# First-layer tiles of one chunk, earlier weight loads, and attention steps held back in the first tile

## The chip, the cores and the metric

The kernel runs on one core of a Trainium2 chip. The metric is the device time of one execution in microseconds (us). In what follows PE is TensorE, DVE is VectorE, ACT is ScalarE, POOL is GpSimd, and SP is the engine that issues all DMA transfers in this kernel, one after the other.

## The reference

A decayed linear attention over chunks feeds two feed-forward layers. Cut to what matters:

```python
# x: (4 batches, 8 heads, 768 positions, 32), a: decay per position, B, C: state of 16
for each chunk of positions:
    M       = (C @ B.T) * exp(cum_i - cum_j) * causal
    y       = M @ x + (C @ state) * exp(cum)
    state   = exp(sum(log a)) * state + sum_j (B_j x_j) * decay_from_j
x = y as 3072 tokens x 256
h = max(x @ w1, x @ w2, x @ w3)          # 256 -> 768
x = h @ w_out                            # 768 -> 256
x = (sigmoid(x @ w_gate) * (x @ w_val)) @ w_out2     # 256 -> 1536 -> 256
```

The four first-layer matrices and the three second-layer matrices arrive as 8-byte floats, viewed as integers, and are decoded on the chip.

## The kernel before

**Attention.** The kernel takes chunks of 96 positions, 8 chunks in all; a chunk of all four batches is 384 tokens. One attention step treats four of the 32 (batch, head) pairs of a chunk, so a chunk has 8 steps and there are 64 steps in all. A step `k` is a product `s` on PE (line 280 for the first two chunks, line 283 later), a multiplication by the decays `mt` (DVE at line 295, or for every second step an ACT copy at 291 and POOL at 292), and a product `y` on PE (line 301). After four steps half a chunk is finished: ACT writes the high part `xt_hi` (line 310), DVE the remainder `xt_lo` (312) and four transposes that carry the state into the next chunk's `xs` (316). The decays of two steps come as one tile `dec`, which is broadcast by a DMA (line 213) into one of four buffers and turned into cumulative products by two scans on DVE (235). From the third chunk on, B and C are split into three bf16 parts (`split_bc`: ACT at 247, POOL at 256) and stored by 12 DMAs into `bi` and `cs` (252).

**First layer.** Tokens are cut into six tiles of 512 columns. A tile has six blocks `m`, and a block has three banks `u` (six matmuls each) and the down product of the block before, `o` (six matmuls). So a tile has 108 `u` and 36 `o` matmuls, each with its own weight load. A block is four slots: one per bank and one for the down product. At the end of every slot `slot_end()` starts attention steps towards a goal, so that the chunks of the next tile are ready in time, and lets waiting work take one stage (`tick`). Between PE's banks run the maxima (ACT 395, DVE 397 and 399), the high part `hi` (ACT 388) and the remainder `lo` (POOL 390).

**Weights.** Each block `m` has two pieces, `raw_a` m0 and m1, of two DMAs of 256 KB (line 127). A piece is decoded by three ACT instructions (141, 143, 144), two on DVE (`t_a` at 148, `r_a` at 150), a cast on ACT (155) and a subtraction on POOL (157). The first block of the first tile can't run before the first two pieces are decoded, and so on through the tile; later tiles find all 12 pieces in place. `BEHIND` says how many pieces are put on SP's queue behind which `dec`. By the page a `dec` is 388 KB, a chunk's `xs` 512, `bx` 256 and `bc` 448 KB, and the stores of a chunk's parts are six of 128 KB (`bi`) and six of 96 KB (`cs`).

**Order.** Every engine runs its instructions in the order that a scheduler gave them when the program was built. SP's queue is such an order too: a transfer that waits for a buffer to come free holds back all that stand behind it. `issue_after` tells the scheduler to place an instruction behind another one. The first 12 steps (`START`) run ahead of the first tile.

**Second layer.** Six tiles of 512, 12 blocks each, lines as in the first layer with `w_b`. It is the same in both kernels.

Of the kernel before, what the change touches and what calls it, by code (L numbers as in the profile page):

```python
# [7 lines left out]
F32 = mybir.dt.float32  # L8
F32R = mybir.dt.float32r
# [9 lines left out]
CH = 96  # L19
# [4 lines left out]
NT = NB * S  # L24
TT = 512
NTT = NT // TT
DM = NH * D
KD = DM // 128
FF1, FF2 = 768, 1536
# [8 lines left out]
TERMS = [(0, 0), (0, 1), (0, 2), (1, 0), (1, 1), (2, 0)]  # L38
KT = 16 * len(TERMS)
DEC = 512  # L40
START = 12
FIRST = 2 * NG
MASKED = 8
LEAD = 2
MTS = 5
DECS = 4

BEHIND = {4: 1, 5: 1, 6: 2, 7: 2, 8: 2, 9: 1, 10: 1, 11: 1, 12: 1}


class Pipe:
# [15 lines left out]
def scan_attention_then_ffn(ctx: ExitStack, tc: tile.TileContext, xh, ah, bch, pick, bn, w1, w2, w3,  # L67
# [170 lines left out]
    def split_bc(c):  # L238

        r = awk.tile([128, BW + 384], F32, tag="bc", bufs=1, name=f"bc{c}")  # L240
        sp.dma_start(out=r, in_=bch[:, c])
        parts = awk.tile([128, 3, BW + 384], BF16, tag="parts", bufs=1, name=f"parts{c}")
        cs[c] = awk.tile([KT, NU, CH], BF16, tag="cs", name=f"cs{c}")
        yield
        for p in range(3):
            with tc.issue_after(evict[0].ins) if c > 2 else ExitStack():
                act.copy(parts[:, p], r)
            for k, (dst, cols) in enumerate(((bi[c % 2], slice(0, BW)),
                                             (cs[c], slice(BW, BW + 384)))):
                for t, pr in enumerate(TERMS):  # L250
                    if pr[k] == p:
                        sp.dma_start(  # L252
                            out=dst[16 * t:16 * t + 16].rearrange("n (g q) i -> n g (q i)", q=4),
                            in_=parts[:, p, cols])
            if p < 2:
                pool.tensor_tensor(out=r, in0=r, in1=parts[:, p], op=ALU.subtract)
            yield splits if p == 2 else None
# [6 lines left out]

    def need(t):

        return 4 * -(-(t + 1) * TT // (2 * CH))

    def attention(k, ahead):

        c, g = steps[k]
        m = mt[k % MTS]
        if k < FIRST:
            ck = cm[:, k % MASKED]
            act.mul(ck.rearrange("p q i -> p (q i)"), bcf[c][:, BW:], pk[:, g:g + 1])
        ps = psu.tile([128, 4, 128], F32, tag="up", name=f"s{c}_{g}")
        for q in range(4):
            u = 4 * g + q
            if k < FIRST:
                pe.matmul(ps[:, q, 0:CH], bcf[c][:, 128 * q:128 * q + 128], ck[:, q],  # L280
                          start=True, stop=True)
            else:
                pe.matmul(ps[:, q, 0:CH], bi[c % 2][:, u, :], cs[c][:, u, :],  # L283
                          start=True, stop=True)
        for _ in range(ahead + 1):
            yield
        dc = dec[k // 2][:, 4 * (g % 2):4 * (g % 2) + 4]
        pool.tensor_tensor(out=m[:, :, CH:CH + N], in0=bx[c][:, 4 * g:4 * g + 4, :],
                           in1=dc[:, :, CH:LW].to_broadcast([128, 4, N]), op=ALU.mult)
        if k >= 4 and k % 2 == 0:  # L290
            act.copy(m[:, :, 0:CH], ps[:, :, 0:CH])
            pool.tensor_tensor(out=m[:, :, 0:CH], in0=m[:, :, 0:CH], in1=dc[:, :, 1:LW],
                               op=ALU.mult)
        else:
            last[0] = dve.tensor_tensor(out=m[:, :, 0:CH], in0=ps[:, :, 0:CH], in1=dc[:, :, 1:LW],
                                        op=ALU.mult)
        prepare(k)
        yield
        y = ys[g // 4]
        for q in range(4):  # L300
            pe.matmul(y[32 * q:32 * q + 32, g % 4, 0:CH + N], xs[c][:, 4 * g + q, :], m[:, q, :],  # L301
                      start=True, stop=True)
        if g % 4 == 3:
            yield
            h = g // 4
            o = (c * CP + 2 * CH * h) % RING
            src = y[:, :, 0:CH].rearrange("p (b k) i -> p b k i", k=KD)
            hi, lo = (v[:, :, o:o + 2 * CH].rearrange("p k (b i) -> p b k i", b=2)
                      for v in (xt_hi, xt_lo))
            act.copy(hi, src)  # L310
            yield
            dve.tensor_tensor(out=lo, in0=src, in1=hi.bitcast(F32), op=ALU.subtract)  # L312
            if c + 1 < NC:
                for q in range(4):
                    rows = slice(32 * q, 32 * q + 32)
                    dve.transpose(
                        out=xs[c + 1][rows, 16 * h:16 * h + 16, :].rearrange(
                            "p (g q) d -> p g q d", q=4)[:, :, q, :],
                        in_=y[rows, :, CH:128])

    def prepare(k):

        c, g = divmod(k, NG)
        if g == 0 and 0 < c < NC - 1:
            load_x(c + 1)
            splits.append(split_bc(c + 1))
        if splits and next(splits[0], None) is splits:
            splits.pop()
        n = k // 2
        if k % 2 == 0:  # L330
            if 5 <= n + 4 < NC * NP:
                load_decay(n + 4, ad)
        elif k < 9:
            decay(n + 1, n == 0)
        else:
            for i in ([n + 1] if k == 9 else []) + [n + 2]:
                if i < NC * NP:
                    with tc.issue_after(last[0].ins) if k > FIRST else ExitStack():
                        decay(i)

    def att_step(ahead=0):
# [12 lines left out]
    acc = {}  # L354

    def down(t, m, mn, w, hl, finish):
        if m == 0:
            acc[t] = [psos[t % len(psos)].tile([128, TT], F32, tag=f"o{d}", name=f"o{mn}_{t}_{d}")
                      for d in range(KD)]
        first = len(w) - KD  # L360
        for d in range(KD):
            three(acc[t][d], [m], mn, w, lambda k: first + d, lambda k: hl[0], lambda k: hl[1])
        if m == mn - 1:
            pipe.add(finish(t, acc[t]))

    def finish1(t, ps):
        yield
        for d in range(KD):
            act.copy(y1[:, d, t * TT:(t + 1) * TT], ps[d])

    def finish2(t, ps):
        yield
# [39 lines left out]
        chain.tick()  # L412
        pipe.tick()

    def layer(t, m, w, n, stages):

        o = (t * TT) % RING
        s = tmpp.tile([128, TT], F32, tag="s", bufs=3, name=f"s{n}_{t}_{m}")
        hl = [tmpp.tile([128, TT], F32R, tag=h, name=f"{h}{n}_{t}_{m}") for h in ("hi", "lo")]
        banks = []  # L420
        for j in range(n):
            ps = psu.tile([128, TT], F32, tag="up", name=f"u{n}_{t}_{m}_{j}")
            three(ps, range(KD), KD, w, lambda k: KD * j + k,
                  lambda k: xt_hi[:, k, o:o + TT], lambda k: xt_lo[:, k, o:o + TT])
            banks.append(ps)
            if j == 0:
                chain.add(stages(s, banks, hl))
            yield hl
# [9 lines left out]
    next(store_all, None)  # L438
    load_x(0, slice(0, 16))
    load_decay(1, ah)  # L440
    load_decay(2, ad)
    load_x(0, slice(16, 32))
    sp.dma_start(out=bcf[1], in_=bch[:, 1])
    load_decay(3, ad)
    load_x(1, slice(0, 16))
    load_decay(4, ad)
    decay(0, clip=True)
# [15 lines left out]

    def slot_end():
        t, s = divmod(slot, slots)
        if t + 1 < NTT:
            goal = need(t) + (need(t + 1) - need(t)) * (s + 1) / (slots - 5)
            while done[0] < min(goal, need(t + 1)):
                for _ in range(2 if t > 1 else 1):
                    att_step(1 if t > 1 else 0)  # L470
        tick()
        weights_tick(t < NTT - 1 or s % 3 == 2)

    for t in range(NTT):
        for m in range(M1):
            for hl in layer(t, m, wt1[m], 3, most):
                slot_end()
                slot += 1
            if pend is not None:
                down(*pend)  # L480
            slot_end()
            slot += 1
            pend = (t, m, M1, wt1[m], hl, finish1)
            if t == NTT - 1 and m == 0:
                actx.close()
                wp2.append(ctx.enter_context(tc.tile_pool(name="wp2", bufs=1)))
                psos.append(ctx.enter_context(tc.tile_pool(name="pso2", bufs=1, space=PSUM)))
                todo += [(piece2, m, part) for m in range(M2) for part in range(2)]
                while todo:
                    load_weights()  # L490
            if t == NTT - 1 and m in (2, 4):
                pipe.add(split_y(m // 2 - 1))


# [1 line left out]
    order += [(t, m) for t in range(2, NTT) for m in range(M2)]  # L496
    for t, m in order:
        eng = pool if t < 2 else dve
        for hl in layer(t, m, wt2[m], 2, lambda s, b, h: gated(s, b, h, eng)):
            tick()  # L500
            slot += 1
            weights_tick(slot % 3 == 2)
# [77 lines left out]
```

## Time and profile before

| | |
|---|---|
| median of three runs | 581.92 us (579.84 to 582.04) |
| the profiled execution's own time | 582.93 us |
| its span, first to last instruction | 581.1 us |
| PE busy | 560.9 us, 97% of the span |
| DVE busy | 312.7 us, 54% |
| ACT busy | 260.7 us, 45% |
| POOL busy | 197.8 us, 34% |
| DMA | 50.52 MB |

A matmul's busy time in the profile is longer than the distance to the next matmul, because matmuls overlap; so a busy PE isn't a PE at its peak, and distances between starts are the better measure. Between the span and the device time lie 1.8 us in which no instruction of the program runs. The shares are averages over very different stages: about the first 90 us are the start, with attention, weight decoding and the first tile together; then comes the rest of the first layer, and from 281 us the second layer.

### The profile page before, as it was taken

To read this page: it belongs to the slowest core of one execution; us is meant where nothing else is said; L and a number is where in the kernel's file an instruction comes from. 1 tells how busy PE (TensorE), PEld (TensorE's weight loads), DVE (VectorE), ACT (ScalarE), POOL (GpSimd) and SP (SyncE) were. 2 spreads that over 40 slices of the span, in tenths; PEclk is the share of its full clock that TensorE was granted. 3 is DMA by queue.
4 is the path that set the end of the run, shared out by engine and by line. 5 is a ranking of instruction groups with operands and counts; after the bars stand their busy time and mean duration, and the time that the engine had idled before them with its cause. 6 is when DMAs were issued, how large, how long until landed. Compare 5 with 4: busy or idle time off the path is not lost.

```text
span 581.1 us, 8016 instructions
## 1 busy us (share of the span) xinstructions
PE 560.9 (97%) x2992; PEld 448.7 (77%) x2992; DVE 312.7 (54%) x455; ACT 260.7 (45%) x475; POOL 197.8 (34%) x219
## 2 busy tenths in 40 slices
PE   4988799999999999999999999999999999999997
PEld 4766567677777777788888888888888888888885
DVE  3879995655857754345766664243343333333332
ACT  4677645225344333256967675442333233232322
POOL 3566965427556523234665555310000000000000
PEclk9998999999999999999999999999999999999999
DMA  7999876827875800395000000010000001000000
GB/s 243 335 241 259 222 153 111 174 65 134 196 162 142 156 2 0 94 363 195 2 1 2 0 2 0 1 72 1 1 7 30 1 0 38 0 1 36 1 0 36
DMA packets 35366, 50.52 MB, mean 87 GB/s; under 512 B 3456, under 2 KB 24320, under 8 KB 35328
## 3 DMA queue, kind: packets, MB, share of 16 engines
q1 hardware_dynamic: 35328, 50.02, 33.4%
q8 instruction: 23, 0.38, 0.3%
q14 instruction: 15, 0.12, 0.1%
HBM read 38.51 MB, written 3.25 MB: 72 GB/s over the span
## 4 chain that ended last, share of the span: by engine, by line
PE 87%; DMA 6%; DVE 3%; issue 1%; SPq 1%; ACT 1%; POOL 0%; DVEq 0%; ACTq 0%; POOLq 0%
PE u L350 19%; PE u L351 18%; PE u L352 18%; PE o L351 8%; PE o L350 8%; PE o L352 8%; PE s L280 3%; PE y L301 3%; DMA raw_a<-in_w 3%; PE s L283 1%; DMA dec<-in_ah 1%; DMA cs<-parts 1%; DMA raw_a<-in_wo 1%; DVE dec L235 1%; SPq L252 0%
## 5 line engine op out<-in xcount | busy, mean ns | idle before, releaser
L388 ACT CAST hi<-s 128x512 fp32r<-128x512 f32 x108 | 67.1, 621 | 181.1 <-DVE s L406 132.1
L390 POOL TENSOR_TENSOR lo<-s,hi 128x512 fp32r<-128x512 f32 x60 | 80.9, 1348 | 95.3 <-ACT hi L388 92.3
L350 PE MATMUL u<-xt_hi,w_b 128*128 128x512 f32 x288 | 112.0, 389 | 0.0
L351 PE MATMUL u<-xt_lo,w_b 128*128 128x512 f32 x288 | 112.0, 389 | 0.0
L352 PE MATMUL u<-xt_hi,w_b 128*128 128x512 f32 x288 | 112.0, 389 | 0.0
L406 DVE TENSOR_TENSOR s<-u,s 128x512 f32<-128x512 f32 x72 | 49.6, 689 | 103.8 <-PE u L352 101.7
L350 PE MATMUL u<-xt_hi,w_a 128*128 128x512 f32 x216 | 89.1, 413 | 2.9 <-DVE s L399 2.0
L351 PE MATMUL u<-xt_lo,w_a 128*128 128x512 f32 x216 | 85.5, 396 | 0.1
L352 PE MATMUL u<-xt_hi,w_a 128*128 128x512 f32 x216 | 85.0, 394 | 0.0
L352 PEld LDWEIGHTS u<-xt_hi,w_b 128*128 128x128 f32 x288 | 54.1, 188 | 11.3
L350 PEld LDWEIGHTS u<-xt_hi,w_b 128*128 128x128 f32 x288 | 54.1, 188 | 11.2
L351 PEld LDWEIGHTS u<-xt_lo,w_b 128*128 128x128 f32 x288 | 54.0, 188 | 11.2
L235 DVE TENSOR_TENSOR_SCAN dec<-dec,delta 128x388 f32<-128x388 f32 x64 | 57.9, 945 | 1.7 <-DMA dec<-ad 1.5
L351 PE MATMUL o<-lo,w_b 128*128 128x512 f32 x144 | 56.1, 390 | 0.0
L352 PE MATMUL o<-hi,w_b 128*128 128x512 f32 x144 | 56.0, 389 | 0.0
L350 PEld LDWEIGHTS u<-xt_hi,w_a 128*128 128x128 f32 x216 | 41.2, 191 | 14.7 <-DVE s L399 2.5
L390 DVE TENSOR_TENSOR lo<-s,hi 128x512 fp32r<-128x512 f32 x48 | 33.2, 692 | 32.5 <-ACT hi L388 32.4
L352 PEld LDWEIGHTS u<-xt_hi,w_a 128*128 128x128 f32 x216 | 41.1, 190 | 9.1
L351 PEld LDWEIGHTS u<-xt_lo,w_a 128*128 128x128 f32 x216 | 41.1, 191 | 8.3 <-DVE xt_lo L312 0.6
L404 ACT ACTIVATE s<-u 128x512 f32<-128x512 f32 x72 | 43.1, 599 | 3.6 <-PE u L352 3.0
L350 PE MATMUL o<-hi,w_b 128*128 128x512 f32 x144 | 44.4, 390 | 0.1
L397 DVE TENSOR_TENSOR s<-u,s 128x512 f32<-128x512 f32 x36 | 24.8, 688 | 35.7 <-PE u L352 32.8
(60 smaller groups left out, 769.7 us busy)
## 6 DMA issues: line engine op xcount, KB each, us to landing
dec<-ad SPq DMA_DIRECT2D x30, 388.0 KB, 5.2
raw_a<-in_w SPq DMA_DIRECT2D x18, 256.0 KB, 7.2
bi<-parts SPq DMA_DIRECT2D x36, 128.0 KB, 5.3
cs<-parts SPq DMA_DIRECT2D x36, 96.0 KB, 5.2
xs<-in_xh SPq DMA_DIRECT2D x6, 512.0 KB, 4.5
raw_b<-in_wg SPq DMA_DIRECT2D x12, 256.0 KB, 5.8
raw_b<-in_wv SPq DMA_DIRECT2D x12, 256.0 KB, 5.8
raw_b<-in_wo SPq DMA_DIRECT2D x12, 256.0 KB, 5.8
```

The source lines that it names most:

```text
L235: dve.tensor_tensor_scan(out=f, data0=f, data1=delta.rearrange("p u w -> p (u w)"), initial=0.0, op0=ALU.mult, op1=ALU.add)
L280: pe.matmul(ps[:, q, 0:CH], bcf[c][:, 128 * q:128 * q + 128], ck[:, q], start=True, stop=True)
L283: pe.matmul(ps[:, q, 0:CH], bi[c % 2][:, u, :], cs[c][:, u, :], start=True, stop=True)
L301: pe.matmul(y[32 * q:32 * q + 32, g % 4, 0:CH + N], xs[c][:, 4 * g + q, :], m[:, q, :], start=True, stop=True)
L350: pe.matmul(ps, wlo, a_hi(k), start=k == 0, stop=False)
L351: pe.matmul(ps, whi, a_lo(k), start=False, stop=False)
L352: pe.matmul(ps, whi, a_hi(k), start=False, stop=k == kn - 1)
L388: act.copy(hl[0], s)
L390: eng.tensor_tensor(out=hl[1], in0=s, in1=hl[0].bitcast(F32), op=ALU.subtract)
L397: dve.tensor_tensor(out=s, in0=banks[1], in1=s, op=ALU.max)
L404: evict[0] = act.activation(out=s, in_=banks[0], func=AF.Sigmoid)
L406: evict[1] = dve.tensor_tensor(out=s, in0=banks[1], in1=s, op=ALU.mult)
```

## The change

The first layer's tiles become seven: four of 384 tokens (one chunk each) and then three of 512. `START` falls from 12 steps to 8, since the first tile needs the first chunk alone. Two weight pieces are put on SP's queue ahead of the second chunk's data, and `BEHIND` puts the ten others behind `dec4` to `dec9` (before, 12 behind `dec4` to `dec12`). In the first tile no attention step starts in the first six slots; the 8 steps of the second chunk are spread over the slots behind. Steps go in pairs, one slot further ahead, from the fourth tile on (before, from the third). Some ACT casts and DVE scans are placed behind other instructions: the casts of `split_bc` behind the latest copy out of PSUM for all chunks, and the scans behind the latest `mt` from the tenth step on.

```diff
+TILES = [(CP * c, CP) for c in range(4)] + [(4 * CP + TT * c, TT) for c in range(3)]
+NT1 = len(TILES)
-START = 12
+START = 8
-BEHIND = {4: 1, 5: 1, 6: 2, 7: 2, 8: 2, 9: 1, 10: 1, 11: 1, 12: 1}
+BEHIND = {4: 1, 5: 1, 6: 2, 7: 2, 8: 2, 9: 2}
...
-            with tc.issue_after(evict[0].ins) if c > 2 else ExitStack():
+            with tc.issue_after(evict[0].ins):
                 act.copy(parts[:, p], r)
...
-        return 4 * -(-(t + 1) * TT // (2 * CH))
+        return 4 * -(-sum(TILES[t]) // (2 * CH))
...
-            act.copy(m[:, :, 0:CH], ps[:, :, 0:CH])
+            evict[0] = act.copy(m[:, :, 0:CH], ps[:, :, 0:CH])
...
-            act.copy(hi, src)
+            evict[0] = act.copy(hi, src)
...
-                    with tc.issue_after(last[0].ins) if k > FIRST else ExitStack():
+                    with tc.issue_after(last[0].ins) if k > 9 else ExitStack():
                         decay(i)
...
-            act.copy(y1[:, d, t * TT:(t + 1) * TT], ps[d])
+            o, n = TILES[t]
+            act.copy(y1[:, d, o:o + n], ps[d])
...
-    load_decay(2, ad)
     load_x(0, slice(16, 32))
-    sp.dma_start(out=bcf[1], in_=bch[:, 1])
+    load_decay(2, ad)
+    load_weights()
     load_decay(3, ad)
+    sp.dma_start(out=bcf[1], in_=bch[:, 1])
+    load_weights()
     load_x(1, slice(0, 16))
     load_decay(4, ad)
...
-        if t + 1 < NTT:
-            goal = need(t) + (need(t + 1) - need(t)) * (s + 1) / (slots - 5)
+        if t + 1 < NT1:
+            goal = need(t) + (need(t + 1) - need(t)) * max(s + 1 - (0 if t else 6), 0) / (
+                slots - 5 - (0 if t else 6))
             while done[0] < min(goal, need(t + 1)):
-                for _ in range(2 if t > 1 else 1):
-                    att_step(1 if t > 1 else 0)
+                for _ in range(2 if t > 2 else 1):
+                    att_step(1 if t > 2 else 0)
...
-    for t in range(NTT):
+    for t in range(NT1):
         for m in range(M1):
-            for hl in layer(t, m, wt1[m], 3, most):
+            for hl in layer(TILES[t], m, wt1[m], 3, most):
                 slot_end()
```

On PE, at the start of the first tile, before the change: in the names, `s1_3` is the `s` of chunk 1 and step 3 of that chunk, `xs1` says that a `y` belongs to chunk 1, and `u3_0_0_0` is tile 0, block 0, bank 0.

```order
L280 MATMUL s0_7_257<-y1_91 128x96 x4
L301 MATMUL y1_104<-mt4_102,xs0_142 32x112 x4
L280 MATMUL s1_0_272<-y1_91 128x96 x4
L301 MATMUL y1_104<-mt0_98,xs0_142 32x112 x4
L280 MATMUL s1_1_298<-y1_91 128x96 x4
L280 MATMUL s1_2_312<-y1_91 128x96 x4
L301 MATMUL y1_104<-mt1_99,xs0_142 32x112 x4
L301 MATMUL y1_104<-mt2_100,xs0_142 32x112 x4
L280 MATMUL s1_3_341<-y1_91 128x96 x4
L301 MATMUL y0_103<-mt3_101,xs1_155 32x112 x4
...
L350 MATMUL u3_0_0_0_482<-xt_hi_92,w_a00_420 128x512
L280 MATMUL s1_4_500<-y1_91 128x96 x4
```

The same place of the changed kernel:

```order
L283 MATMUL s0_7_263<-y1_91 128x96 x4
L304 MATMUL y1_104<-mt4_102,xs0_142 32x112 x4
L304 MATMUL y1_104<-mt0_98,xs0_142 32x112 x4
L304 MATMUL y1_104<-mt1_99,xs0_142 32x112 x4
L304 MATMUL y1_104<-mt2_100,xs0_142 32x112 x4
L354 MATMUL u3_0_0_0_388<-xt_hi_92,w_a00_326 128x384
L354 MATMUL u3_0_0_1_401<-xt_hi_92,w_a00_326 128x384
L354 MATMUL u3_0_0_2_412<-xt_hi_92,w_a01_336 128x384
```

The four `s` and four `y` of chunk 1 no longer stand ahead of the first `u`; the first of them now stands behind the second block's last bank.

On SP, the last weight pieces of the first tile, before the change: `dec9` is the tenth decay tile, `parts2` are the split parts of chunk 2, and `xs3`, `bx3`, `bc3` are data of chunk 3.

```order
L213 DMA dec9_383<-ad_105 128x776
L127 DMA raw_a40_385<-in_w1 128x2x256
L127 DMA raw_a40_385<-in_w2 128x2x256
L252 DMA bi0_96<-parts2_330 16x8x512
L252 DMA cs2_331<-parts2_330 16x8x384
L224 DMA bx3_656<-in_bn 128x512
L241 DMA bc3_659<-in_bch 128x896
L213 DMA dec10_522<-ad_105 128x776
L127 DMA raw_a41_524<-in_w3 128x2x256
L127 DMA raw_a41_524<-in_wo1 128x512
L213 DMA dec11_587<-ad_105 128x776
L127 DMA raw_a50_589<-in_w1 128x2x256
```

The same place of the changed kernel:

```order
L255 DMA bi0_96<-parts2_474 16x8x512
L216 DMA dec8_476<-ad_105 128x776
L130 DMA raw_a40_478<-in_w1 128x2x256
...
L130 DMA raw_a41_481<-in_wo1 128x512
L255 DMA bi0_96<-parts2_474 16x8x512 x2
L255 DMA cs2_475<-parts2_474 16x8x384 x3
L255 DMA bi0_96<-parts2_474 16x8x512 x2
L255 DMA cs2_475<-parts2_474 16x8x384 x2
L216 DMA dec9_571<-ad_105 128x776
L130 DMA raw_a50_573<-in_w1 128x2x256
...
L130 DMA raw_a51_576<-in_wo1 128x512
```

The last pieces, a50 and a51, now stand ahead of chunk 3's data and of `dec10` and `dec11`, but still behind nine stores of chunk 2's parts and behind `dec9`, which waits for a buffer that step 11 sets free.

## Rows read from the trace of the kernel before

**Rows 1.** Stretches: PE, PEld, DVE, ACT, POOL busy; granted clock, DMA share, GB/s.

```profile
41.20:90.40 49.20, 43.08 (x282) 31.18 (x283) 45.27 (x63) 30.60 (x55) 36.21 (x35) 0.97 0.90 216
281.40:577.00 295.60, 295.45 (x1302) 244.03 (x1301) 130.24 (x170) 124.01 (x231) 53.13 (x44) 1.00 0.03 10
```

**Rows 2.** PE in order of time: 108th `u` matmul, then layer 2's first.

```profile
90.37 0.39 PE L352 MATMUL u<-xt_hi,w_a 128*128 128x512 f32 x1
...
281.42 0.39 PE L350 MATMUL u<-xt_hi,w_b 128*128 128x512 f32 x1
```

**Rows 3.** Chain that ended last, around 45 us: start, length, what.

```profile
37.56 7.88 DMA raw_a<-in_w
...
45.46 7.45 DMA raw_a<-in_w
...
52.93 5.79 DMA raw_a<-in_wo
```

**Rows 4.** PE groups by shape, 90.8 to 281.4 us: busy, mean ns, idle before.

```profile
L352 PE MATMUL u<-xt_hi,w_a 128*128 128x512 f32 x180 | 70.3, 390 | 0.0
L352 PE MATMUL o<-hi,w_a 128*128 128x512 f32 x62 | 24.4, 394 | 0.0
L283 PE MATMUL s<-cs,bi 96*128 96x96 bf16 x160 | 12.7, 208 | 0.3 <-DVE s L397 0.3
L301 PE MATMUL y<-mt,xs 128*32 128x112 f32 x320 | 12.6, 266 | 0.0
```

**Rows 5.** PE and its weight loads in order of time, at 42, 53 and 401 us.

```profile
41.79 0.63 PE L352 MATMUL u<-xt_hi,w_a 128*128 128x512 f32 x1
42.22 0.63 PE L350 MATMUL u<-xt_hi,w_a 128*128 128x512 f32 x1
...
53.20 1.03 PE L280 MATMUL s<-y 128*128 128x96 f32 x8
...
401.10 0.39 PE L352 MATMUL o<-hi,w_b 128*128 128x512 f32 x1
401.10 0.19 PEld L351 LDWEIGHTS o<-lo,w_b 128*128 128x128 f32 x1
401.32 0.39 PE L351 MATMUL o<-lo,w_b 128*128 128x512 f32 x1
```

**Rows 6.** DVE in order of time around the first tile's start.

```profile
34.27 0.56 DVE L295 TENSOR_TENSOR mt<-s,dec 128x384 f32<-128x384 f32 x1 [2.30 <-PE s L280]
...
40.59 0.55 DVE L312 TENSOR_TENSOR xt_lo<-y,xt_hi 128x384 fp32r<-128x384 f32 x1
```

**Rows 7.** DVE groups by shape, 41.2 to 90.4 us.

```profile
L150 DVE CUSTOM_DVE_ANT_0 r_a<-t_a,r_a 128x1024 uint16<-128x1024 uint16 x9 | 11.0, 1236 | 0.8 <-ACT raw_a L143 0.5
L235 DVE TENSOR_TENSOR_SCAN dec<-dec,delta 128x388 f32<-128x388 f32 x12 | 10.9, 943 | 0.0
L148 DVE SCALAR_TENSOR_TENSOR t_a<-raw_a,sg 128x512 int32<-128x512 int32 x9 | 10.5, 1167 | 1.1 <-DMA cs<-parts 1.1
L316 DVE STREAM_TRANSPOSE xs<-y 32x128 f32<-32x128 f32 x14 | 4.3, 309 | 0.1
```

**Rows 8.** Weight pieces: duration ns least, median, greatest; time to landing.

```profile
L148 DVE SCALAR_TENSOR_TENSOR t_a<-raw_a,sg x12: 681/1074/1769, 25.8 to 79.2; 128x512 int32<-128x512 int32 x12
L150 DVE CUSTOM_DVE_ANT_0 r_a<-t_a,r_a x12: 666/933/2168, 30.2 to 83.8; 128x1024 uint16<-128x1024 uint16 x12
...
DMA to landing us min/median/max: 4.0/7.3/9.9
```

**Rows 9.** ACT and POOL groups of the weight pieces, 41.2 to 90.4 us.

```profile
L155 ACT CAST w_a<-r_a 128x512 fp32r<-128x512 f32 x10 | 6.2, 620 | 12.2 <-DVE r_a L150 12.2
L157 POOL TENSOR_TENSOR w_a<-r_a,w_a 128x512 fp32r<-128x512 f32 x10 | 13.7, 1375 | 5.7 <-ACT w_a L155 5.7
```

**Rows 10.** DMA in the first 80 us.

```profile
DMA packets 14220, 20.25 MB, mean 253 GB/s; under 512 B 1445, under 2 KB 10012, under 8 KB 14213
```

**Rows 11.** The stretch of the third tile, columns as in the first group.

```profile
129.70:169.80 40.10, 39.81 (x290) 30.69 (x289) 26.50 (x45) 17.00 (x29) 24.06 (x28) 1.00 0.83 168
```

More of the change, by code (lines that the diff above doesn't have):

```diff
@@ L333, in prepare @@
         elif k < 9:
-            decay(n + 1, n == 0)
+            with tc.issue_after(last[0].ins) if k > 9 else ExitStack():
+                decay(n + 1, n == 0)
         else:
@@ L337, in prepare @@
                 if i < NC * NP:
-                    with tc.issue_after(last[0].ins) if k > FIRST else ExitStack():
+                    with tc.issue_after(last[0].ins) if k > 9 else ExitStack():
                         decay(i)
@@ L356, in down @@
     def down(t, m, mn, w, hl, finish):
+        n = hl[0].shape[1]
         if m == 0:
-            acc[t] = [psos[t % len(psos)].tile([128, TT], F32, tag=f"o{d}", name=f"o{mn}_{t}_{d}")
+            acc[t] = [psos[t % len(psos)].tile([128, TT], F32, tag=f"o{d}", name=f"o{mn}_{t}_{d}")[:, 0:n]
                       for d in range(KD)]
@@ L413, in tick, with layer @@
         pipe.tick()
[L415 to L419, printed above, removed]
+    def layer(tile, m, w, n, stages):
+        o, size = tile
+        name = f"{n}_{o}_{m}"
+        r = slice(o % RING, o % RING + size)
+        s = tmpp.tile([128, TT], F32, tag="s", bufs=3, name=f"s{name}")[:, 0:size]
+        hl = [tmpp.tile([128, TT], F32R, tag=h, name=f"{h}{name}")[:, 0:size] for h in ("hi", "lo")]
         banks = []
         for j in range(n):
-            ps = psu.tile([128, TT], F32, tag="up", name=f"u{n}_{t}_{m}_{j}")
+            ps = psu.tile([128, TT], F32, tag="up", name=f"u{name}_{j}")[:, 0:size]
             three(ps, range(KD), KD, w, lambda k: KD * j + k,
-                  lambda k: xt_hi[:, k, o:o + TT], lambda k: xt_lo[:, k, o:o + TT])
+                  lambda k: xt_hi[:, k, r], lambda k: xt_lo[:, k, r])
             banks.append(ps)
@@ L440, in scan_attention_then_ffn @@
     load_decay(1, ah)
+    load_x(0, slice(16, 32))
     load_decay(2, ad)
-    load_x(0, slice(16, 32))
+    load_weights()
+    load_decay(3, ad)
     sp.dma_start(out=bcf[1], in_=bch[:, 1])
-    load_decay(3, ad)
+    load_weights()
     load_x(1, slice(0, 16))
@@ L465, in slot_end @@
         t, s = divmod(slot, slots)
-        if t + 1 < NTT:
-            goal = need(t) + (need(t + 1) - need(t)) * (s + 1) / (slots - 5)
+        if t + 1 < NT1:
+            goal = need(t) + (need(t + 1) - need(t)) * max(s + 1 - (0 if t else 6), 0) / (
+                slots - 5 - (0 if t else 6))
             while done[0] < min(goal, need(t + 1)):
-                for _ in range(2 if t > 1 else 1):
-                    att_step(1 if t > 1 else 0)
+                for _ in range(2 if t > 2 else 1):
+                    att_step(1 if t > 2 else 0)
         tick()
-        weights_tick(t < NTT - 1 or s % 3 == 2)
-    for t in range(NTT):
+        weights_tick(t < NT1 - 1 or s % 3 == 2)
+    for t in range(NT1):
         for m in range(M1):
-            for hl in layer(t, m, wt1[m], 3, most):
+            for hl in layer(TILES[t], m, wt1[m], 3, most):
                 slot_end()
@@ L483, in scan_attention_then_ffn @@
             pend = (t, m, M1, wt1[m], hl, finish1)
-            if t == NTT - 1 and m == 0:
+            if t == NT1 - 1 and m == 0:
                 actx.close()
@@ L490, in scan_attention_then_ffn @@
                     load_weights()
-            if t == NTT - 1 and m in (2, 4):
+            if t == NT1 - 1 and m in (2, 4):
                 pipe.add(split_y(m // 2 - 1))
@@ L498, in scan_attention_then_ffn @@
         eng = pool if t < 2 else dve
-        for hl in layer(t, m, wt2[m], 2, lambda s, b, h: gated(s, b, h, eng)):
+        for hl in layer((t * TT, TT), m, wt2[m], 2, lambda s, b, h: gated(s, b, h, eng)):
             tick()
```

## The prediction, made before the changed kernel had run

> **What bounds the kernel now.** I read the page first: PE is busy nearly throughout, so time can only be won where PE waits or where it does less. The stretches then say where. In the second layer PE issues 1302 matmuls in 295.6 us, 0.227 us each, and nothing else in that stretch is near its limit [rows 1]. From 41.2 to 90.4 us it is different: DVE is busy 45.27 of 49.20 us, the DMA engines 90%, POOL 36.21 us, and PE issues only 282 matmuls [rows 1]. The chain that ended last runs there through waits for weight pieces, 7.88, 7.45 and 5.79 us one behind the other [rows 3]. That stretch is the first tile; its 108th and last `u` matmul starts at 90.37 us [rows 2].
>
> From 90.6 us on PE sets the time. Up to the second layer's first matmul at 281.42 us [rows 2] it has 540 `u` (three groups of 180), 186 `o` (three of 62) and 40 attention steps (320 records of `y`, eight to a step; 160 of `s`, four to a step) [rows 4]. The 726 matmuls at 0.227 take 164.8 us, so a step costs PE (190.8 - 164.8) / 40 = 0.65 us, its switches included. Idle ahead of PE is under half a microsecond in every group there [rows 4]. So two questions decide: how much PE work is left when the first tile ends, and when it ends.
>
> **What is left behind the first tile.** A matmul of 384 columns doesn't occur before. While the first tile starts, matmuls of 512 columns are 0.43 us apart (41.79 to 42.22), which is 512 columns at the 1.2 GHz level; later 0.22 to 0.23 (401.10 to 401.32) [rows 5], which is 0.213 us at 2.4 GHz and some 14 ns. Either the 14 ns are fixed (0.174 us at 384) or they go with the columns (0.170). I take 0.174. The columns in all are the same, so this alone costs 576 x 0.174 against 432 x 0.227: 2 us more, or nothing.
>
> When the changed kernel has streamed its 108th `u`, by its order 30 `o` and 16 steps are done. Left up to the second layer are 438 narrow matmuls (76.2 us), 426 wide ones (96.7 us) and 48 steps at 0.65 (31.2 us): 204.1 us. Before, it is 190.8 us from 90.6. So the change breaks even if its first tile's `u` end at 281.4 - 204.1 = 77.3 us (78.9 with 0.170); each microsecond earlier is one gained. The second layer and the end are the same.
>
> **When the first tile starts.** DVE ends the `xt_lo` that the steady flow of `u` waits for at 41.1 us [rows 6]. Ahead of it go away: four scans (0.943 each, 3.8 us), four transposes (1.2) [rows 7], one `xt_lo` and two `mt` (1.6) [rows 6], one `r_a` (0.7 to 1.2) [rows 7, 8], together 7.4 us; and a wait of 2.30 us for an `s` of the second chunk [rows 6]. That gives 31.3 us. That the two weight pieces now overtake the second chunk's data on SP costs nothing there: these data are wanted only by step 8, behind the second block; if the cover were gone, it would be a landing, 7.3 us [rows 8].
>
> **When it ends, by DVE.** From there to the last piece's `r_a` DVE has 10 `r_a` and 9 `t_a`, 8 scans (7.5), 8 transposes (2.5), one `xt_lo` (0.55), 4 `mt` and 10 maxima over 384 columns (0.56 each, the price of an `mt` of that size [rows 6], 7.8): 18.4 us without the weights. `t_a` and `r_a` took 1.167 and 1.236 us in the crowded stretch [rows 7], but 0.68 and 0.67 at the least [rows 8]: 22.9 us against 12.8. Behind the last `r_a` follow a cast 0.62, a subtraction 1.375 [rows 9] and six matmuls, 3.0 us. So the tile's `u` end between 31.3 + 31.2 + 3.0 = 65.5 and 75.6 us. The first three of the ten pieces are decoded before the tile's own maxima and remainders load POOL and DVE, so I take three at the low price and seven at the high one: 72.6 us.
>
> **By transfers.** Up to and with the last piece SP issues 15.35 MB: 24 weight transfers of 256 KB, 10 `dec` of 388 KB, ten stores of parts (1.1 MB), and 3.9 MB of x, B and C for the first chunks. At the 253 GB/s of the first 80 us [rows 10] they end at 60.7 us if the queue never stands still. Three ACT instructions (at the cast's 0.62), `t_a`, `r_a`, cast and subtraction make 6.3 us more [rows 7, 9], six matmuls 1.0: 68 us. So DVE's bound is the later one, unless SP stands still.
>
> **The later tiles.** The fourth narrow tile takes 12 steps, as a wide one did before. Transfers then filled 0.83 x 40.1 = 33.3 us [rows 11]; the narrow tile's PE work is 144 x 0.174 + 12 x 0.65 = 32.9 us. I add 0.4 us; it is nothing if buffers were filled in the lighter tile ahead, and 4.1 us if the DMA engines can't go over the 90% of the start [rows 1]. The new places of casts and scans, and pairs of steps from the fourth tile on, I cost at nothing: beyond the first tile DVE and ACT have slack (26.50 and 17.00 of 40.10 us [rows 11]), and without it a late `mt` would show as PE's waits, now 0.4 us and less per group [rows 4].
>
> **The sum.** 582.93 - (77.3 - 72.6) + 0.4 = 578.6 us against the profiled execution. That execution was 1.0 us over the median of the runs, so I forecast 577.6 us.
>
> **Rivals.** (a) *Transfers alone bind.* If `t_a` and `r_a` mostly run at their low price, the tile ends at 68 us and matmuls cost 0.170: 9 to 11 us gained, 571.5 to 573 us. For it: these instructions are short whenever POOL is quiet [rows 8]; against: POOL has the same ten subtractions in less time.
> (b) *The start is won and spent in the first tile.* All ten pieces at the high price, 75.6 us: 580.6 us, no change that can be told. Runs of one kernel lie within 0.4% here, so 0.5% (2.9 us) is about what can be told from none. This is also the case in which the earlier weights do nothing, because DVE decodes them no sooner.
> (c) *The last pieces come a landing later, and it is slower.* a50 and a51 stand behind nine stores of parts and behind `dec9`, which waits for step 11, and that step can't start before the sixth slot. Before, pieces were waited for in just this way [rows 3]. One landing more, 7.3 us [rows 8], ends the tile at 79.9: 584.9 us; the longest, 9.9, 587.5. It decides from 79.8 us on. Against: the queue is shorter by a chunk's data than before.
> (d) *Narrow matmuls don't shrink.* A weight load lasts 0.19 us [rows 5], more than 0.174; if the next matmul waited for its end, 438 matmuls would lose 16 ns each, 7 us: 584.6 us. Against: the eight `s` matmuls in 1.03 us, with a load each, are 0.13 us apart at most [rows 5].
> The Trainium skill speaks against narrow tiles here (TensorE: Matmul & The Clock Gate, The mechanism): a weight load overlaps matmuls in flight only if it uses another row group. All loads here use all rows, so by that rule load and stream would add up, and 144 loads more would cost some 27 us. The trace disagrees at 512 columns: the load at 401.10 lies inside the 0.22 us between two matmuls [rows 5]. I leave that rule a hundredth within (d).
>
> **How the numbers follow.** The forecast's own case, the tile ending between 69.5 and 75 us, has 0.52 (574 to 579 us); up to 74.0 it is faster by over 0.5%, which is 0.45 of it. (a) has 0.12, (b) 0.18, (c) 0.12, (d) 0.06. Faster is 0.45 + 0.12 = 0.57, the same 0.07 + 0.18 = 0.25, slower 0.18. The range, 571.5 to 584.5, goes from (a) with the cheaper matmul to the crowded price with the 4.1 us of the fourth tile; it leaves out most of (c) and (d).
>
> **What would show it.** The first steady `u` near 31 us; the 108th `u` near 72.6, with DVE busy over nine tenths in between; 384-column matmuls 0.174 us apart; SP standing at the store ahead of `dec8` until ACT has cast chunk 2's first part; no PE idle to speak of behind the first tile. The prediction is wrong if the 108th `u` comes after 77 us, if PE shows idle ahead of `u` at the last two blocks of more than some 5 us, or if PE waits for attention in the narrow tiles.

## The result, and the profile after

The changed kernel takes 588.38 us (median of four runs, 587.57 to 589.34); beside it on the same chip the kernel before takes 581.74 (579.84 to 582.04). The ratio is 1.013, 95% interval 1.011 to 1.015: slower by 6.6 us, where 577.6 was forecast. The profiled execution took 587.57 us, its span is 585.8.

First PE in order of time: the first `u` of the steady flow, four matmuls that follow each other, the 108th `u`, and the second layer's first matmul. [rows 2] and [rows 5] hold their counterparts.

```profile
31.10 0.69 PE L355 MATMUL u<-xt_lo,w_a 128*128 128x384 f32 x1 [1.99 <-DVE xt_lo L315]
...
45.16 0.33 PE L356 MATMUL o<-hi,w_a 128*128 128x384 f32 x1
45.33 0.33 PE L355 MATMUL o<-lo,w_a 128*128 128x384 f32 x1
45.51 0.33 PE L356 MATMUL o<-hi,w_a 128*128 128x384 f32 x1
45.68 0.33 PE L354 MATMUL u<-xt_hi,w_a 128*128 128x384 f32 x1
...
76.53 0.33 PE L356 MATMUL u<-xt_hi,w_a 128*128 128x384 f32 x1
...
286.10 0.39 PE L354 MATMUL u<-xt_hi,w_b 128*128 128x512 f32 x1
```

The first tile starts 10 us earlier than before and ends 13.8 us earlier, but the second layer starts 4.7 us later. So behind the first tile lie 286.10 - 76.53 = 209.6 us, where the forecast had 204.1, and the first tile ends 3.9 us behind its forecast of 72.6. These two make the result: against the break-even of 77.3 the tile won 0.8 us, the rest lost 5.5, and 582.93 - 0.8 + 5.5 = 587.6, the profiled time.

The two stretches in which that happens, the first tile and the fourth, with the columns of [rows 1]:

```profile
31.10:76.70 45.60, 39.29 (x263) 34.62 (x264) 39.27 (x56) 29.85 (x54) 30.86 (x29) 0.93 0.67 176
137.90:174.40 36.50, 32.55 (x286) 29.54 (x285) 24.95 (x45) 15.46 (x29) 22.23 (x28) 0.95 0.87 163
```

In the first tile no engine is full: DVE 86%, the DMA engines 67%, where before it was 92% and 90% [rows 1]. Something stands. It is SP, in order of time (start, length, line, transfer):

```profile
31.58 0.34 SPq L227 DMA_DIRECT2D xs<-in_xh  x1
45.83 0.68 SPq L255 DMA_DIRECT2D bi<-parts  x1
46.60 0.52 SPq L216 DMA_DIRECT2D dec<-ad  x1
47.18 2.54 SPq L130 DMA_DIRECT2D raw_a<-in_w  x3
49.76 0.47 SPq L130 DMA_DIRECT2D raw_a<-in_wo  x1
50.27 1.22 SPq L255 DMA_DIRECT2D bi<-parts  x2
51.53 1.93 SPq L255 DMA_DIRECT2D cs<-parts  x3
53.56 2.15 SPq L255 DMA_DIRECT2D bi<-parts  x2
56.66 1.23 SPq L255 DMA_DIRECT2D cs<-parts  x2
58.12 0.40 SPq L216 DMA_DIRECT2D dec<-ad  x1
58.58 1.60 SPq L130 DMA_DIRECT2D raw_a<-in_w  x3
```

Between 31.92 and 45.83 SP issues nothing. The first store of chunk 2's parts waits for the cast that ACT makes at 44.83, and behind it in the queue stand `dec8`, a40 and a41, then nine more stores, `dec9`, a50 and a51. The store is not all that holds a40: `dec8` goes into the buffer that steps 8 and 9 read, and by POOL in order of time step 8's `mt` reads it until 46.18:

```profile
45.04 1.14 POOL L295 TENSOR_TENSOR mt<-mt,dec 128x384 f32<-128x384 f32 x1 [0.21 <-ACT mt L294]
```

Without the store, `dec8` could have gone only some 0.4 us earlier than it did. What SP waits for is the held steps, as e4 below shows. The chain of waits (start, length, what) goes through the second transfer of a41:

```profile
49.76 6.88 DMA raw_a<-in_wo
56.73 0.78 ACT sg L144
```

ACT in order of time shows the cast that held the queue, and what ACT did when a41 landed:

```profile
44.83 0.97 ACT L250 CAST parts<-bc 128x896 bf16<-128x896 f32 x1
...
56.73 0.78 ACT L144 ACTIVATE sg<-raw_a 128x512 f16<-128x512 f32 x1 [2.18 <-DMA raw_a<-in_wo]
```

PE in order of time shows who pays, here and later:

```profile
58.53 0.66 PE L354 MATMUL u<-xt_hi,w_a 128*128 128x384 f32 x1 [2.47 <-ACT s L401]
58.99 0.52 PE L355 MATMUL u<-xt_lo,w_a 128*128 128x384 f32 x1
59.31 0.52 PE L356 MATMUL u<-xt_hi,w_a 128*128 128x384 f32 x1
...
160.32 0.33 PE L286 MATMUL s<-cs,bi 96*128 96x96 bf16 x4 [3.95 <-DMA bc<-in_bch]
...
162.56 0.52 PE L354 MATMUL u<-xt_hi,w_a 128*128 128x384 f32 x1
162.88 0.52 PE L355 MATMUL u<-xt_lo,w_a 128*128 128x384 f32 x1
```

ACT idles 2.18 us for a41's transfer; the copy that frees PE's bank (`s`, line 401) stands behind a41's decoding in ACT's order, and PE waits 2.47 us for it. The row at 160.32 is the other loss: the first `s` of chunk 5, in the fourth tile, waits 3.95 us for the chunk's stored parts, and after it `u` matmuls stand 0.32 us apart instead of 0.173. PE's waits behind the first tile (engine, line, released by; us in total, times, longest) are one row:

```profile
PE s L286 <- DMA bc<-in_bch: 4.0, 1, 4.0
```

How long the parts take is read from ACT in order of time, the three casts of chunk 5:

```profile
140.90 0.95 ACT L250 CAST parts<-bc 128x896 bf16<-128x896 f32 x1
144.80 0.93 ACT L250 CAST parts<-bc 128x896 bf16<-128x896 f32 x1
149.97 0.95 ACT L250 CAST parts<-bc 128x896 bf16<-128x896 f32 x1
```

and from SP's last two stores of them:

```profile
151.18 0.56 SPq L255 DMA_DIRECT2D bi<-parts  x1
151.79 0.59 SPq L255 DMA_DIRECT2D cs<-parts  x1
```

PE came to the `s` 3.95 us before it could start it, at 156.4, 15.5 us behind the first cast; the parts were there after 19.4, of which the last store's way, with the DMA engines 87% busy, is 8.5. In the kernel before, the same chain had 20.4 us, from ACT's first cast of chunk 5,

```profile
132.20 0.94 ACT L247 CAST parts<-bc 128x896 bf16<-128x896 f32 x1
```

to PE's first `s` of it, the 97th of the 192 matmuls of line 283, which has no wait:

```profile
152.56 0.34 PE L283 MATMUL s<-cs,bi 96*128 96x96 bf16 x4
```

The named releaser, the load of the next `bc`, is what the profile infers; the stores ahead of it on SP's queue are what `s` reads.

### The profile page after: what moved, and what is told of

The parts are those of the page before. It is cut to its first block, busy times and chain, and to the rows that moved or that the text cites. A ratio compares the mean times of both kernels' runs of the same rounds, so it can differ in the third digit from the quotient of the medians.

```text
span 585.8 us, 8342 instructions
## 1 busy us (share of the span) xinstructions
PE 555.7 (95%) x3136; PEld 461.6 (79%) x3136; DVE 307.0 (52%) x467; ACT 263.6 (45%) x489; POOL 198.7 (34%) x225
## 4 chain that ended last, share of the span: by engine, by line
PE 85%; DMA 8%; SPq 2%; ACT 2%; DVE 1%; issue 1%; POOL 1%; ACTq 0%; POOLq 0%; DVEq 0%
PE u L354 19%; PE u L355 18%; PE u L356 18%; PE o L355 8%; PE o L354 8%; PE o L356 8%; PE y L304 2%; DMA xs<-in_xh 2%; PE s L286 1%; DMA raw_a<-in_w 1%; DMA raw_a<-in_wo 1%; DMA bi<-parts 1%; DMA bc<-in_bch 1%; DMA dec<-ad 1%; SPq L255 1%
## 5 line engine op out<-in xcount | busy, mean ns | idle before, releaser
L394 ACT CAST hi<-s 128x512 fp32r<-128x512 f32 (+1 forms) x114 | 68.2, 598 | 192.8 <-DVE s L412 137.0
L396 POOL TENSOR_TENSOR lo<-s,hi 128x512 fp32r<-128x512 f32 (+1 forms) x66 | 84.5, 1280 | 98.0 <-ACT hi L394 93.6
L412 DVE TENSOR_TENSOR s<-u,s 128x512 f32<-128x512 f32 x72 | 49.8, 692 | 125.2 <-PE u L356 119.9
L354 PE MATMUL u<-xt_hi,w_a 128*128 128x384 f32 (+1 forms) x252 | 95.6, 381 | 7.2 <-ACT s L401 2.5
L355 PE MATMUL u<-xt_lo,w_a 128*128 128x384 f32 (+1 forms) x252 | 92.1, 365 | 2.0 <-DVE xt_lo L315 2.0
L356 PE MATMUL u<-xt_hi,w_a 128*128 128x384 f32 (+1 forms) x252 | 91.7, 364 | 0.0
L354 PEld LDWEIGHTS u<-xt_hi,w_a 128*128 128x128 f32 x252 | 48.4, 192 | 16.4 <-issue 3.6
L355 PEld LDWEIGHTS u<-xt_lo,w_a 128*128 128x128 f32 x252 | 48.6, 193 | 6.5 <-DVE xt_lo L315 2.5
L356 PEld LDWEIGHTS u<-xt_hi,w_a 128*128 128x128 f32 x252 | 48.4, 192 | 4.4
L403 DVE TENSOR_TENSOR s<-u,s 128x384 f32<-128x384 f32 (+1 forms) x42 | 25.6, 610 | 37.1 <-PE u L356 36.0
```

What stands on the lines that cost most here:

```text
L354: pe.matmul(ps, wlo, a_hi(k), start=k == 0, stop=False)
L355: pe.matmul(ps, whi, a_lo(k), start=False, stop=False)
L356: pe.matmul(ps, whi, a_hi(k), start=False, stop=k == kn - 1)
L394: act.copy(hl[0], s)
L396: eng.tensor_tensor(out=hl[1], in0=s, in1=hl[0].bitcast(F32), op=ALU.subtract)
L403: dve.tensor_tensor(out=s, in0=banks[1], in1=s, op=ALU.max)
```

## The experiments

Each starts from the changed kernel. Times are medians; the ratio is to the kernel before in the same set of runs (581.07 us for e1 to e4, 580.33 for e5 to e8, 581.32 for e10 to e13). The last three columns come from PE in order of time in the profiled execution, which can lie up to 1.4 us off the median: the 108th `u`, the second layer's first matmul, and the distance between them, in which every wait behind the first tile lies.

| run | us | ratio (95%) | 108th `u` | layer 2 | between |
|---|---|---|---|---|---|
| changed kernel | 588.38 | 1.013 (1.011 to 1.015) | 76.53 | 286.10 | 209.6 |
| e1_spread | 582.62 | 1.004 (1.002 to 1.005) | 76.03 | 280.70 | 204.7 |
| e2_ahead | 585.65 | 1.010 (1.007 to 1.013) | 73.63 | 284.09 | 210.5 |
| e3_both | 580.90 | 1.000 (0.999 to 1.002) | 73.80 | 279.54 | 205.7 |
| e4_nohold | 584.55 | 1.007 (1.005 to 1.009) | 72.58 | 283.42 | 210.8 |
| e6_nohold_spread | 579.48 | 0.998 (0.996 to 0.999) | 71.73 | 277.02 | 205.3 |
| e5_cast | 585.71 | 1.008 (1.005 to 1.011) | 74.01 | 283.94 | 209.9 |
| e7_noscan | 575.34 | 0.991 (0.989 to 0.993) | 67.92 | 273.68 | 205.8 |
| e8_moved | 583.75 | 1.005 (1.003 to 1.006) | 78.59 | 283.63 | 205.0 |
| e10_nohold_spread_ahead | 578.31 | 0.996 (0.994 to 0.997) | 70.79 | 276.54 | 205.8 |
| e11_singles | 585.06 | 1.007 (1.005 to 1.010) | 77.16 | 283.94 | 206.8 |
| e12_nohold_spread_cast | 580.62 | 0.999 (0.998 to 1.000) | 73.50 | 279.54 | 206.0 |
| e13_late | 592.27 | 1.019 (1.017 to 1.022) | 80.56 | 291.46 | 210.9 |

The theory behind the first four: two losses that have nothing to do with each other, SP standing in the first tile (about 4 us), and chunk 5's parts wanted too soon in the fourth (about 5 us). The rival: both come out of one crowded transfer queue, so that relief at one place is paid at the other.

**e1_spread**: the steps of the second to fourth tile are asked for 10, 10 and 8 at a time, not 8, 8 and 12.

```diff
-        return 4 * -(-sum(TILES[t]) // (2 * CH))
+        return (8, 16, 26, 36, 44, 56, 64)[t]
```

> Changed kernel, but the 20 steps of tiles 2 and 3 are spread as 10, 10 and 8 over tiles 1, 2 and 3 instead of 8, 8 and 12. Theory: in the fourth narrow tile 12 steps follow each other so closely that the parts of chunk 5 (cast at 140.9 us, stored by 12 DMAs) land only at 160 us while PE wants them at 156; this cost 4.0 us of waiting and 1.7 us of half clock behind it. Spread, that wait goes: 582 to 583.5 us, no idle of PE over 1 us between 77 and 286 us. Rival, the DMA engines are simply full in the narrow tiles (busy 0.92 there) and the wait only moves to another tile: 587 to 589 us.

582.62 us, as expected. PE has no wait of 0.1 us or more behind the first tile, and the stretch there falls by 4.9 us to 204.7. The first tile ends where it did, so that loss is separate.

**e2_ahead** and **e3_both**: pieces a30 to a51 all stand behind `dec7`, ahead of the stores of chunk 2; in e3 with the steps spread as well.

```diff
-BEHIND = {4: 1, 5: 1, 6: 2, 7: 2, 8: 2, 9: 2}
+BEHIND = {4: 1, 5: 1, 6: 2, 7: 6}
```

> Changed kernel, but the last four weight pieces stand behind dec7, ahead of the store of chunk 2's parts at which SP stood for 14.0 us. Theory: SP's standing made a40 to a51 land late; the first tile's last u (76.5 us) comes 3 to 5 us earlier and the whole takes 583.5 to 585.5 us. Rival, DVE's decoding sets the first tile's end whatever SP does: last u at 75 to 76.5 us and 587.5 to 589 us in all.

> Both edits together. If both theories hold they add up: 577.5 to 580.5 us, faster than before. If only the spread counts 582 to 583.5, if only the weights 583.5 to 585.5, if neither 587 to 589 us.

585.65 and 580.90 us, a little over what was expected. SP still stands 9.1 us at the store, but no weights are behind it any more, and the 108th `u` comes 2.9 us earlier. The wait in the fourth tile (3.7 us) stays in e2. In e3 DVE is then nearly full from 31 to 74 us, with the clock up:

```profile
31.00:74.00 43.00, 36.87 (x258) 33.11 (x259) 41.48 (x57) 29.11 (x54) 31.65 (x30) 1.00 0.69 182
```

**e4_nohold**: the steps of the second chunk start at the first slot.

```diff
-            goal = need(t) + (need(t + 1) - need(t)) * max(s + 1 - (0 if t else 6), 0) / (
-                slots - 5 - (0 if t else 6))
+            goal = need(t) + (need(t + 1) - need(t)) * (s + 1) / (
+                slots - 5)
```

> Changed kernel with attention steps from the first slot of the first tile (undoes the hold of six slots alone). Theory that SP stands for the store which waits for step 8: the store and dec8 are issued some 5 us earlier, a41 lands near 52 instead of 56.7 us, and the total falls by 1 to 3 us, to 585.5 to 587.5. Rival, that the hold keeps PE, ACT and DVE free for the first blocks: the first tile's first blocks come later and the total is 589 to 591 us.

584.55 us: a larger gain than expected, 3.8 us. SP's order shows why. Step 8 begins `split_bc` for chunk 2 and issues `dec8`, step 10 issues `dec9`, and each drags its weight pieces along; with the steps held, so are the pieces. Without the hold:

```profile
31.81 1.99 SPq L255 DMA_DIRECT2D bi<-parts  x3
...
40.62 0.34 SPq L216 DMA_DIRECT2D dec<-ad  x1
41.01 1.46 SPq L130 DMA_DIRECT2D raw_a<-in_w  x3
...
49.62 1.46 SPq L130 DMA_DIRECT2D raw_a<-in_w  x3
```

`dec8` now goes at 40.62, when step 9's `mt` on DVE (40.02 and 0.54) has let go of its buffer, although the first six stores were issued long before. a40 is issued at 41.01 instead of 47.18, a50 at 49.62 instead of 58.58, and the 108th `u` is at 72.58. A wait of 4.5 us in the fourth tile stays.

**e6_nohold_spread**: e4 and e1 together.

> The hold of six slots undone, and the steps of the narrow tiles spread 10, 10, 8. If the two losses are separate (SP standing still in the first tile, the parts of chunk 5 wanted too early in the fourth), their gains of 3.8 and 5.8 us add up: 578 to 580 us, the 108th u near 72.6 and the second layer's first matmul near 278. If both come out of one queue of transfers, so that what is taken from one place is paid at the other, it gives the larger gain alone: 582 to 583 us.

579.48 us: the two gains add up, the second layer starts at 277.02. The rival of one crowded queue falls.

**e5_cast**: only the casts of chunk 2 go back to where they were.

```diff
-            with tc.issue_after(evict[0].ins):
+            with tc.issue_after(evict[0].ins) if c > 2 else ExitStack():
                 act.copy(parts[:, p], r)
```

> Only the place of the casts of chunk 2's parts undone: they are no longer put behind the latest copy out of PSUM, and all twelve stores of chunk 2 then stand on SP ahead of dec8 and a40. If what costs in the first tile is that a store waits for a cast that ACT does late, the wait shrinks and the 108th u comes at 73 to 75: 584.5 to 586.5 us. If what costs is how much stands on SP ahead of the last four pieces, they come later still, the 108th u at 78 to 81: 589 to 593 us.

585.71 us, the 108th `u` at 74.01: the time of the first case, but not for its reason. SP in order of time, from the last of the twelve stores on:

```profile
43.23 0.60 SPq L255 DMA_DIRECT2D cs<-parts  x1
...
47.80 0.33 SPq L216 DMA_DIRECT2D dec<-ad  x1
48.19 2.96 SPq L130 DMA_DIRECT2D raw_a<-in_w  x3
...
52.06 0.34 SPq L216 DMA_DIRECT2D dec<-ad  x1
52.44 1.68 SPq L130 DMA_DIRECT2D raw_a<-in_w  x3
```

No store stands at the head any more, and still `dec8` goes only at 47.80, when POOL's `mt` of step 8 (46.39 and 1.38) has let go of its buffer; a40 comes 1.0 us later than in the changed kernel. a50 comes 6.1 us earlier, since no stores stand between a41 and it: they went while SP would have stood anyway. So the new place of the casts is worth about 2.5 us of the loss, through the nine stores ahead of a50 and not through the store at which SP stood.

**e7_noscan**: e3 without the scans of `dec5` to `dec8`; the decays of these steps aren't cumulated.

```diff
-            dve.tensor_tensor_scan(out=f, data0=f, data1=delta.rearrange("p u w -> p (u w)"),
-                                   initial=0.0, op0=ALU.mult, op1=ALU.add)
+            if not 5 <= n <= 8:
+                dve.tensor_tensor_scan(out=f, data0=f, data1=delta.rearrange("p u w -> p (u w)"),
+                                       initial=0.0, op0=ALU.mult, op1=ALU.add)
```

> The kernel with the steps spread and the last pieces ahead of the stores, and without the scans of dec5 to dec8 (so the decays of steps 10 to 17 aren't cumulated). Four of these eight scans, 3.6 us of DVE, stand ahead of the last r_a. If DVE is what ends the first tile there (busy 42.3 of 44.0 us), the 108th u moves from 73.8 to 70 to 71 and the time to 576.5 to 578 us. If transfers end it, the 108th u stays at 73 to 74 and the time at 580 to 581 us.

575.34 us, the 108th `u` at 67.92: further than expected. The count in the expectation was wrong: in e3 all eight of these scans stand ahead of the last `r_a` (68.42), the first two of them at 29.21, and here none stands between 29 us and the last `r_a` (61.15). So 7.5 us at 0.94 each are gone, and the tile ends 5.9 us sooner, with DVE then busy 34.40 of the 39 us from 29 to 68. Most of the work taken from DVE comes back, so in e3 DVE, and not the transfers, ends the first tile.

**e8_moved** and **e11_singles** ask why chunk 5's parts are late. My theory was that twelve steps in a narrow tile are enough for it. e8 takes the twelve in the third tile; e11 leaves them in the fourth, but takes them one by one instead of in pairs a slot further ahead.

```diff
-        return 4 * -(-sum(TILES[t]) // (2 * CH))
+        return (8, 16, 24, 36, 44, 56, 64)[t]
```

> The changed kernel with the twelve steps taken in the third narrow tile instead of the fourth (8, 12, 8 in place of 8, 8, 12). If twelve steps in some 33 us are what leaves the parts of a chunk too little time from cast to product, PE's wait of 4 us moves with them: it stands ahead of an s of chunk 4 in the third tile, none over 1 us in the fourth, and the time stays at 586.5 to 589 us. If it is the fourth tile itself (steps in pairs from there on, or transfers that pile up towards it), the third shows no wait over 1 us, the fourth keeps 2 us or more or loses it, and the time is 583 to 587 us.

```diff
-                for _ in range(2 if t > 2 else 1):
-                    att_step(1 if t > 2 else 0)
+                for _ in range(2 if t > 3 else 1):
+                    att_step(1 if t > 3 else 0)
```

> The changed kernel with the pairs of steps, one slot further ahead, from the fifth tile on instead of the fourth. If the pairs, which ask for chunk 5's parts earlier after its first cast, are what makes PE wait in the fourth tile, the wait falls from 4.0 us to under 1, the half clock behind it goes too, and the time is 582 to 584 us. If the twelve steps in one narrow tile are enough for it, 2 us or more of the wait stay and the time is 585.5 to 588.5 us.

The theory fell with e8: no wait over 1 us moves to the third tile. (The first tile of its profiled execution ends 2 us later than in the changed kernel; why stays open.) PE's waits from 78 to 282 us in e8 are small ones:

```profile
PE u L354 <- POOL w_a L160: 0.3, 1, 0.3
PE s L286 <- DMA dec<-ad: 0.2, 1, 0.2
PE u L354 <- DVE s L405: 0.2, 1, 0.2
```

and so are those of e11:

```profile
PE s L286 <- DMA dec<-ad: 0.5, 1, 0.5
PE u L354 <- DVE s L405: 0.2, 1, 0.2
```

It takes both, twelve steps in a narrow tile and the pairs. In e8 chunk 4's first product comes 16.6 us behind that chunk's first cast (111.83 to 128.44) and waits 0.2. In e11 chunk 5's first product comes 16.9 us behind the chunk's first cast and waits 0.53. First and third cast on ACT:

```profile
141.53 0.95 ACT L250 CAST parts<-bc 128x896 bf16<-128x896 f32 x1
...
148.84 0.94 ACT L250 CAST parts<-bc 128x896 bf16<-128x896 f32 x1 [1.54 <-POOL bc L259]
```

and that product on PE:

```profile
158.44 0.33 PE L286 MATMUL s<-cs,bi 96*128 96x96 bf16 x4 [0.53 <-DMA dec<-ad]
```

It is asked for 16.4 us behind the first cast, 0.9 later than with pairs, and the third cast follows the first after 7.3 us, not 9.1. So the pairs shorten the time that the chain has and lengthen the time that it needs. The time, 585.06, is still over what was expected: from the first tile to the second layer e11 needs about 2 us more than e1 and e8. From the last `u` of the third tile to that of the fourth it takes 34.2 us, and e8's third tile, with the same twelve single steps, 34.0; the changed kernel's fourth tile, with pairs, takes 36.5, which without its wait and the matmuls at half the clock behind it would be some 31.6 (an estimate from these rows). So single steps cost PE some 2 us there, and the two waits above 0.7.

**e10_nohold_spread_ahead** and **e12_nohold_spread_cast** look for a version that beats both kernels: e6 with the pieces placed as in e2, and e6 with the casts placed as in e5.

> Hold undone, steps spread 10, 10, 8, and the last pieces (a30 to a51) all behind dec7, ahead of the stores of chunk 2. If DVE ends the first tile once SP's standing is gone (39.2 of 41.0 us busy between 31 and 72 us with the hold undone and the steps spread), earlier pieces bring nothing more: the 108th u at 71 to 73 us, the time 578.5 to 580.5 us. If the last pieces were still late there, the 108th u comes at 68 to 70 and the time is 576 to 578 us.

> Hold undone, steps spread 10, 10, 8, and the casts of chunk 2's parts where they were before the change. If DVE ends the first tile, nothing more is won than with the first two: 578.5 to 580.5 us, the 108th u at 71 to 73. If the casts still made pieces late, 1 to 3 us less, the 108th u at 69 to 71.

e10 is the best of all, 578.31 us, ratio 0.9958 (0.9942 to 0.9974), 3 us under the kernel before. It lies just past the good end of the case in which DVE binds (578.5 us, the 108th `u` at 71) and short of the other, and DVE is busy 98% of the time from 31 to 71 us:

```profile
31.00:71.00 40.00, 36.97 (x251) 32.16 (x252) 39.13 (x56) 28.79 (x53) 32.60 (x30) 0.94 0.78 201
```

e12, 580.62, brings nothing over e6; its first tile ends at 73.50, later than in either case expected, with DVE busy 36.2 of the 42 us from 31 to 73, so DVE isn't what ends it. The casts' old place pays only while the hold is there. Whether it costs without it is not clear, since the intervals of e6 and e12 overlap, and what ends the tile there stays open.

**e13_late**: the two earliest pieces go back behind the second chunk's data.

```diff
-BEHIND = {4: 1, 5: 1, 6: 2, 7: 2, 8: 2, 9: 2}
+BEHIND = {4: 2, 5: 2, 6: 2, 7: 2, 8: 2, 9: 2}
...
-    load_weights()
     load_decay(3, ad)
     sp.dma_start(out=bcf[1], in_=bch[:, 1])
-    load_weights()
```

> The changed kernel with its two earliest weight pieces put back behind the second chunk's data (two pieces behind each of dec4 to dec9). If the first tile's end hangs on the order in which the last pieces stand on SP (which is the same in both), the first u comes at most 2 us later and the 108th stays within 2 us of 76.5: 587 to 590 us. If the two early pieces are what lets the rest of the tile run early, all of it moves by the 3 to 4 us of transfers that now stand ahead of them: the 108th u at 79 to 81 and 590.5 to 593 us.

592.27 us, the 108th `u` at 80.56, the second case. PE's waits from 24 to 82 us begin with decoded pieces that come late, 3.8 us for the longest:

```profile
PE u L354 <- POOL w_a L160: 6.1, 3, 3.8
```

So the early weight loads are a real gain of some 4 us within this change. No run undoes the narrow tiles, `START` or the new place of the scans alone.

## Why the prediction was wrong, step by step

**What failed first: "pairs of steps from the fourth tile on, I cost at nothing", and "I add 0.4 us" for the fourth narrow tile.** Both were priced by how busy DVE, ACT and the DMA engines are, and these did have slack. What ran out was time along one chain: ACT cast, POOL subtraction, ACT cast, twice over, then stores on SP at some 0.6 us each, then a landing. That chain had 20.4 us before; narrow tiles and pairs left it 15.5 where it needed 19.4. Without pairs it has 16.4 and needs 16.9 (e11). The cost was 4.0 us of waiting and about 1 us of matmuls at half the clock behind it; e1 takes both away (204.7), e8 and e11 show which two parts of the change it takes. The prediction did name PE waiting for attention in the narrow tiles as what would make it wrong, but gave it no price and no chance. Its range held 4.1 us for this tile, for DMA engines that can't go over 90%; that this is the size measured is luck, since in e11 the same twelve steps with the same transfers take 34.2 us and not the 37.0 of that case.

**What failed second: "So DVE's bound is the later one, unless SP stands still".** SP stood, 14 us, and in the changed kernel the 108th `u` is at 76.53. In the runs in which DVE is busy 95% or more of the first tile it is at 70.8 to 73.8 (e2, e3, e4, e6, e10). Two things held the last pieces. The held steps keep the buffer of `dec8`, behind which a40 stands: e4, without the hold, ends the tile 4.0 us earlier. And nine stores stand between a41 and a50: e5, without them there, ends it 2.5 us earlier, so the new places of the casts were not to be had at nothing either. Rival (c) named the nine stores and the buffer that a step sets free, but priced them at a full landing (79.9) and held "the queue is shorter by a chunk's data than before" against them. That its totals, 584.9 and 587.5 us, lie near the profiled 587.57 is luck: its tile ends at 79.9 and 82.5.

That 72.6 fits the runs in which DVE binds is partly luck too. In e3 `t_a` and `r_a` together take 23.8 us from the start of the tile to the last `r_a`, where the sum had some 20; but only six scans, nine maxima and three `mt` stand there, where the sum had eight, ten and four, some 3 us less.

**What was right.** The steady `u` start at 31.10 (forecast 31.3, though its terms add up to 31.4). Matmuls of 384 columns are 0.173 to 0.174 us apart, so the 14 ns are fixed rather than in proportion, and rival (d) falls. The Trainium skill's rule (TensorE: Matmul & The Clock Gate, The mechanism), that a load overlaps matmuls in flight only if its row group differs, would add loads to the stream here; the trace disagrees, since a load lasts 0.19 us and the distance is 0.173. The work behind the first tile, 204.1 us, measures 204.7 to 206.0 in the seven kernels that lose that wait and keep the pairs in the fourth tile. The break-even of 77.3 holds with it: by the same sum e1, whose tile ends at 76.03, should take 582.93 - 1.3 + 0.6 = 582.2 us, and its profiled execution took 582.2.

**The rivals.** (a) falls: from 31 to 74 us `t_a` and `r_a` took 1.16 and 1.06 us on average in the changed kernel, well above the 0.68 and 0.67 of the low price, and of all runs only e7, with less DVE work, ends its first tile near 68. (b) was close in its price: in e3 they took 1.25 and 1.27 us, the crowded price for all of them, but what stood on SP and not this price set the end in the changed kernel.

## What to carry to other kernels

When a stage is made shorter, price not only how busy each engine is in it, but every chain that must fit into it: from the first cast to the product here, read from the trace of before as a distance in time, and scaled with the tile and with how far ahead the consumer is issued. When loads are tied to steps of a schedule, holding a step holds its loads and all that stands behind them on the queue; look for what is at the head of the queue and whom it waits for, and then for whom the next one would wait if the head were gone. Gains at different places add up only if each is checked alone: here a start won by 10 us was given back as 4 us to a queue and 5 to a chain, and with both mended (e10) the change is worth some 3 us.

## What the runs showed of the hardware

After PE's waits of 2.47 and 3.95 us, matmuls of 384 columns ran 0.32 us apart, which is the 1.2 GHz level, from 58.2 to 61.6 and from 160.6 to 164.0 us, before they came back to 0.173. The granted clock was 0.50 in both stretches, and 0.95 over the whole fourth tile. Of the 4.9 us between the changed kernel and e1 behind the first tile, 3.95 are the wait, which leaves about 1 us for this. Two more pairs that differ by the spread of the steps alone leave as much: e2 and e3 4.7 us with a wait of 3.74, e4 and e6 5.55 with 4.52. In e1, e3 and e6 the clock was 1.00 throughout behind the first tile. A stall cost more than its own length here.
